# Extra products on TensorE in the first block of a pooled-attention and two-MLP kernel

## The chip, the cores and the metric

The kernel runs on one core of one Trainium2 chip, as one program with one launch. The metric is the device time of that program in microseconds (us): the median of several runs.

## The reference, cut to what matters

```python
# attention: q, k, v are (8, 8, 576, 64); keys and values are means over groups of 8 rows
k_p = k.reshape(B, H, Sp, pool, D).mean(axis=3)          # Sp = 72
v_p = v.reshape(B, H, Sp, pool, D).mean(axis=3)
scores = scale * np.matmul(q, k_p.transpose(0, 1, 3, 2))
attn = softmax(scores)                                    # over the 72 pooled keys
x = np.matmul(attn, v_p)  ->  (4608 tokens, 512)
# first MLP, three parallel inputs, d_ff = 768
h = np.maximum(np.maximum(x @ w1, x @ w2), x @ w3)
x = h @ w_out
# second MLP, d_ff = 2048
h = np.maximum(x @ w_in, 0.0)
return h * h @ w_out2
```

Here `softmax` and the last two names stand for a few lines of the reference. Inputs are float32; the weights of both MLPs come as 64-bit numbers.

## The kernel before, in words

**Tiling.** The 4608 tokens are cut into 12 blocks j of T1 = 384 tokens. For each block the kernel computes the attention of its tokens, which gives four tiles x[0] to x[3] (one for each pair of heads p), and then the first MLP in 22 steps: 18 steps (f, e), one for each of six column chunks f and three input weights e, and four output steps d. Nearly all products are made of split float32: a number is a high and a low part, and a product is three matmuls (high by high, high by low, low by high; PARTS in the code). So a step (f, e) is 4 x 3 = 12 matmuls of 384 columns (L465), and an output step is 18 (L484). The results wait in HBM for the second MLP, which runs after all blocks (L600 and L645).

**Attention of a block.** For each pair p: `prepare` makes the split queries and pooled keys, `softmax` multiplies queries by keys into a PSUM tile `sc` (L344), takes the maximum (VectorE, L346), exponentials (ScalarE, L349) and the division (GpSimd, L355). `transpose` then turns each tile of 128 queries round on TensorE (L370) into the PSUM tile `tr`, from which ScalarE (L372) and VectorE (L373) take the two parts `pt`. `values` multiplies by the pooled values (L385 for the first batch), and ScalarE (L121) and VectorE (L122) write the high and the low part of x[p]. In block 0 the query tiles of a pair start at c = 0, 128 and 256, so there are 12 transposed tiles. Pool `tr_ps` has one place for `tr`; the tile with c = 128 uses the place `av1` instead.

**Weights.** Each of the 18 input weights and six output weights of the first MLP is loaded by SyncE from HBM and turned from 64 bits into float32 with two ScalarE (L148, L149) and two VectorE (L150, L153) instructions, and then split (L121 on ScalarE, L122 on GpSimd). All of this happens while blocks 0 and 1 of the attention are made.

**Order.** Work goes into a list `todo` with a due time and is issued in that order; the attention of block j + 1 is spread over the steps of block j. The framework then places each engine's instructions by a timeline of its own (`schedule_with_timeline_sim=True`), with program order as priority, so an instruction that is ready can move ahead of one that isn't. On the chip every engine takes its instructions strictly in that placed order. `mm_ps` has three PSUM places, so three steps can be open at once.

Of the kernel before, what the change touches and what calls it, by code (L numbers as in the profile page):

```python
# [20 lines left out]
P = 128  # L21
B, H, S, D = 8, 8, 576, 64
POOL = 8
SP = S // POOL
# [8 lines left out]
NE = 3  # L33
# [32 lines left out]
NATURAL = 1  # L66

LIGHT = 2

# [8 lines left out]
def as_f32(ap):  # L80
    return ap.bitcast(F32)
# [3 lines left out]
def attention_moe_kernel(ctx: ExitStack, tc: tile.TileContext, q, k, v, vn, w1, w2, w3, wo1, wi2, wo2, out):  # L85
    nc = tc.nc
# [5 lines left out]
    ident = const.tile([P, P], F32, name="ident")  # L92
# [31 lines left out]
    def split(hl, src, engine=nc.vector):  # L124

        split_to(hl[:, 0], hl[:, 1], src, engine)
# [141 lines left out]
    def score_tiles(n):  # L268
        m = P if n % P == 0 else n // 2
        return [(c, m) for c in range(0, n, m)]  # L270

    def attention(j):
# [5 lines left out]
        for b, s0, n, t in pieces(j):  # L278
# [5 lines left out]
            for p in range(NPAIR):  # L284
# [3 lines left out]
                tiles = score_tiles(n)  # L288
                if j < LIGHT:
                    todo.append((at, functools.partial(softmax, tiles)))  # L290
                for c, m in tiles:
                    if j >= LIGHT:
                        todo.append((at, functools.partial(softmax, [(c, m)])))
# [13 lines left out]
    def attend(j, b, s0, n, p, t):  # L307

        kr, vr, qr, qs, pt, sms = [], [], [], [], [], {}
        first, light = s0 == 0, j < LIGHT  # L310

# [50 lines left out]
        def transpose(c, m):  # L362
            if c == 0:
                pt.append(pt_p.tile([SP, 2, 2, T1], F32R, tag="pt", name="pt"))
            if light and c == m:
                tr = av_ps.tile([P, T1], F32, tag="av1", name="tr")[:SP, : 2 * P].rearrange("s (h q) -> s h q", h=2)
            else:
                tr = tr_ps.tile([SP, 2, P], F32, tag="tr", name="tr")
            for h in range(2):
                nc.tensor.transpose(tr[:, h, :m], sms[c][:, h], ident[:m, :m])  # L370
            hi, lo = pt[0][:, 0, :, c : c + m], pt[0][:, 1, :, c : c + m]
            nc.scalar.activation(hi, tr[:, :, :m], AF.Copy)  # L372
            nc.vector.tensor_tensor(out=lo, in0=tr[:, :, :m], in1=as_f32(hi), op=ALU.subtract)  # L373

        def values():
# [24 lines left out]
            split(x, xf)  # L400

        return load, prepare, softmax, transpose, values

    w1_t, wo1_t = {}, {}
# [48 lines left out]
    def moe1(j):  # L453

        x = x_t.pop(j)
        hs = []
        for f in range(KF1):
            hm = t_p.tile([P, T1], F32, tag="hm", name="hm")
            h = h_p.tile([P, 2, T1], F32R, tag="h", name="h")
            for e in range(NE):  # L460
                ps = mm_ps.tile([P, T1], F32, tag="ps", name="ps")
                n = 0
                for kk in range(KD):
                    for a, c in PARTS:
                        nc.tensor.matmul(  # L465
                            ps, lhsT=w1_t[f, e][:, a, kk * P : (kk + 1) * P], rhs=x[kk][:, c],
                            start=(n == 0), stop=(n == 3 * KD - 1),
                        )
                        n += 1
                if e == 0:  # L470
                    nc.scalar.activation(hm, ps, AF.Copy)
                else:
                    nc.vector.tensor_tensor(out=hm, in0=ps, in1=hm, op=ALU.max)  # L473
                if e == NE - 1:
                    split(h, hm)
                yield
            hs.append(h)
            now[0] = hm
        for d in range(KD):
            ps = mm_ps.tile([P, T1], F32, tag="ps", name="ps")  # L480
            n = 0
            for kk in range(KF1):
                for a, c in PARTS:
                    nc.tensor.matmul(  # L484
                        ps, lhsT=wo1_t[kk][:, a, d * P : (d + 1) * P], rhs=hs[kk][:, c],
                        start=(n == 0), stop=(n == 3 * KF1 - 1),
                    )
                    n += 1
            ys = t_p.tile([P, T1], F32, tag="ys", name="ys")
            nc.scalar.activation(ys, ps, AF.Copy)  # L490
            nc.scalar.dma_start(out=y_dram[j][d], in_=ys)
            yield
# [6 lines left out]
    def add_moe1(j):  # L499
        steps = moe1(j)  # L500
        todo.extend((j * STEPS + i, functools.partial(next, steps, None)) for i in range(STEPS))
# [227 lines left out]
```

## Time and profile before

| | us |
|---|---|
| median of 3 runs | 1546.03 (1545.82 to 1547.47) |
| the profiled execution, its own time | 1546.39 |
| its span, first to last instruction | 1544.7 |
| TensorE busy in the span | 1509.4 (98%) |
| VectorE busy in the span | 948.2 (61%) |
| mean granted TensorE clock | 0.987 of full speed |

The profile is one execution. PE is TensorE, DVE is VectorE, ACT is ScalarE, POOL is GpSimd, SP is SyncE. L465 is line 465 of the kernel. A name such as `ps<-x,w` is the tile written and the tiles read. Times are counted from the span's start. The end of a matmul is modelled and overlaps the next one; the distance between two starts is what one costs in a row of them. A granted clock of 1.00 is 2.4 GHz and 0.50 is 1.2 GHz; those are the only two levels that this trace has. The first clock record is at 11.66 us; a stretch before it is printed as 1.00 whatever the clock was.

### The profile page before, as it was taken

How to read it: one execution, taken by the hardware profiler on the slowest of the kernel's cores; microseconds unless marked ns; L12 is line 12 of the kernel's file. 1: busy time of each engine (PE TensorE's matmuls, PEld its weight loads, DVE VectorE, ACT ScalarE, POOL GpSimd, SP SyncE). 2: the span in 40 equal slices, each digit the busy share in tenths (PEclk: the TensorE clock that was granted, in tenths of full speed). 3: DMA queues.
4: the chain of work that ended last, by engine and by line, in shares of the span. 5: the costliest groups of instructions: out<-in, count | busy, mean ns of one | idle time of the engine just before them, and what ended most of it. 6: DMA issues, size and time to landing. Idle time of an engine off the chain costs nothing.

```text
span 1544.7 us, 25098 instructions
## 1 busy us (share of the span) xinstructions
PE 1509.4 (98%) x9290; PEld 1413.8 (92%) x9290; DVE 948.2 (61%) x1991; ACT 623.5 (40%) x1772; POOL 199.4 (13%) x303
## 2 busy tenths in 40 slices
PE   6899999999999999999999999999999999999998
PEld 4789999999999999999999898988989888999987
DVE  6895678776776767755427555455655546464544
ACT  7875566656666556654212212121212112121211
POOL 5541122222222121322000000000000000000000
PEclk7799999999999999999999999999999999999999
DMA  7552234434334332323475424333333433343331
GB/s 226 159 172 68 76 105 149 145 95 143 122 119 143 97 132 99 102 77 123 135 289 208 150 109 164 110 121 123 112 137 124 150 123 108 111 150 109 137 109 69
DMA packets 80858, 200.87 MB, mean 130 GB/s; under 512 B 9024, under 2 KB 32576, under 8 KB 80736
## 3 DMA queue, kind: packets, MB, share of 16 engines
q1 hardware_dynamic: 73824, 189.83, 36.1%
q10 hardware_dynamic: 6912, 9.44, 1.7%
q8 instruction: 74, 1.21, 0.3%
q14 instruction: 48, 0.39, 0.1%
HBM read 157.29 MB, written 41.94 MB: 129 GB/s over the span
## 4 chain that ended last, share of the span: by engine, by line
PE 85%; DVE 5%; DMA 5%; ACT 2%; issue 2%; SPq 0%; POOL 0%; DVEq 0%; ACTq 0%; POOLq 0%
PE ps L465 25%; PE acc L645 25%; PE ps L600 21%; PE ps L484 9%; PE sc L344 2%; DMA out_dram<-o 2%; PE tr L370 2%; DMA wraw<-in_w_dram 1%; PE av L396 1%; PE av L395 1%; DVE wbits L153 1%; DMA vr<-in_v_dram 1%; DMA wraw<-in_wo_dram 1%; DMA kq<-in_k_dram 1%; DVE wbits L150 0%
## 5 line engine op out<-in xcount | busy, mean ns | idle before, releaser
L465 PE MATMUL ps<-x,w 128*128 128x384 f32 x2592 | 507.6, 343 | 1.8 <-DVE x L122 1.0
L465 PEld LDWEIGHTS ps<-x,w 128*128 128x128 f32 x2592 | 451.1, 191 | 3.9 <-DVE x L122 2.0
L645 PE MATMUL acc<-wo2s,g 128*128 128x512 f32 x1728 | 412.5, 391 | 0.0
L600 PEld LDWEIGHTS ps<-y,wi2s 128*128 128x128 f32 x3024 | 370.4, 188 | 12.5 <-PE ps L600 3.4
L600 PE MATMUL ps<-y,wi2s 128*128 128x256 f32 x3024 | 376.8, 280 | 2.8 <-DVE s L629 2.2
L645 PEld LDWEIGHTS acc<-wo2s,g 128*128 128x128 f32 x1728 | 316.2, 188 | 62.6
L121 ACT ACTIVATE g<-c 128x512 fp32r<-128x512 f32 x144 | 90.8, 630 | 410.4 <-DVE c L611 403.6
L617 DVE TENSOR_TENSOR s<-ps,s 128x512 f32<-128x512 f32 x72 | 49.8, 692 | 262.2 <-PE ps L600 261.6
L484 PE MATMUL ps<-h,wo 128*128 128x384 f32 x864 | 165.2, 339 | 0.5 <-DVE hm L473 0.4
L484 PEld LDWEIGHTS ps<-h,wo 128*128 128x128 f32 x864 | 148.9, 188 | 1.3 <-DVE hm L473 0.7
L617 DVE TENSOR_TENSOR c<-ps,s 128x512 f32<-128x512 f32 x144 | 99.0, 688 | 24.9 <-PE ps L600 21.7
L355 POOL TENSOR_TENSOR ss<-ss,st 128x144 f32<-128x144 f32 (+3 forms) x144 | 74.2, 517 | 308.7 <-DVE st L354 238.6
L473 DVE TENSOR_TENSOR hm<-ps,hm 128x384 f32<-128x384 f32 x144 | 79.5, 552 | 54.2 <-PE ps L465 50.3
L349 ACT ACTIVATE ss<-sc,st 128x72 f32<-128x72 f32 (+1 forms) x320 | 98.3, 314 | 33.3 <-DVE st L346 30.8
L122 DVE TENSOR_TENSOR g<-c,g 128x512 fp32r<-128x512 f32 x144 | 98.8, 686 | 17.3 <-ACT g L121 16.4
L611 DVE SCALAR_TENSOR_TENSOR c<-c 128x512 f32<-128x512 f32 x144 | 99.0, 688 | 2.2
L373 DVE TENSOR_TENSOR pt<-tr,pt 72x256 fp32r<-72x256 f32 (+1 forms) x160 | 61.5, 387 | 52.6 <-ACT pt L372 51.2
L344 PEld LDWEIGHTS sc<-kbd,qs 128*128 128x128 f32 (+1 forms) x480 | 73.3, 191 | 12.3 <-issue 5.3
L344 PE MATMUL sc<-kbd,qs 128*128 128x144 f32 (+1 forms) x480 | 73.9, 269 | 9.2 <-ACT kbd L195 5.3
L372 ACT ACTIVATE pt<-tr 72x256 fp32r<-72x256 f32 (+1 forms) x160 | 56.4, 355 | 58.9 <-PE tr L370 57.4
L370 PE MATMUL tr<-ident,ss 128*72 128x128 f32 (+1 forms) x320 | 59.2, 271 | 13.9 <-DVE pt L373 8.8
L349 ACT ACTIVATION_READ_ACCUMULATOR ss<-sc,st 128x1 f32 (+1 forms) x320 | 63.4, 198 | 0.0
(78 smaller groups left out, 1247.0 us busy)
## 6 DMA issues: line engine op xcount, KB each, us to landing
wo2s<-wo_dram SPq DMA_DIRECT2D x144, 512.0 KB
wi2s<-wi_dram SPq DMA_DIRECT2D x24, 512.0 KB
wraw<-in_wo_dram SPq DMA_DIRECT2D x22, 512.0 KB
wraw<-in_w_dram SPq DMA_DIRECT2D x18, 512.0 KB
y_dram<-ys ACTq DMA_DIRECT2D x48, 192.0 KB
out_dram<-o SPq DMA_DIRECT2D x36, 256.0 KB
wraw<-in_wi_dram SPq DMA_DIRECT2D x16, 512.0 KB
wi_dram<-wraw SPq DMA_DIRECT2D x16, 512.0 KB
```

What stands on the lines that cost most here:

```text
L121: nc.scalar.activation(hi, src, AF.Copy)
L122: engine.tensor_tensor(out=lo, in0=src, in1=as_f32(hi), op=ALU.subtract)
L344: nc.tensor.matmul(src[:, i], lhsT=lhsT, rhs=kbd[:, p, l], start=(n == 0), stop=(n == 2))
L349: nc.scalar.activation(ss[:, i, h], src[:, i, h], AF.Exp, bias=st[:, 0, i, h : h + 1], accum_out=st[:, 1, i, h : h + 1],)
L370: nc.tensor.transpose(tr[:, h, :m], sms[c][:, h], ident[:m, :m])
L465: nc.tensor.matmul(ps, lhsT=w1_t[f, e][:, a, kk * P : (kk + 1) * P], rhs=x[kk][:, c], start=(n == 0), stop=(n == 3 * KD - 1),)
L473: nc.vector.tensor_tensor(out=hm, in0=ps, in1=hm, op=ALU.max)
L484: nc.tensor.matmul(ps, lhsT=wo1_t[kk][:, a, d * P : (d + 1) * P], rhs=hs[kk][:, c], start=(n == 0), stop=(n == 3 * KF1 - 1),)
L600: nc.tensor.matmul(bank[:, u * HT : (u + 1) * HT], lhsT=wi2_t[2 * gr + u][i][:, a, o + kk * P : o + (kk + 1) * P], rhs=y_t[j][m][:, c, kk] ...
L611: nc.vector.scalar_tensor_tensor(out=c, in0=c, scalar=0.0, in1=c, op0=ALU.max, op1=ALU.mult)
L617: nc.vector.tensor_tensor(out=c, in0=bank, in1=other, op=ALU.add)
L645: nc.tensor.matmul(acc_t[j][2 * half + i], lhsT=g[:, a, u * HT + i * P : u * HT + (i + 1) * P], rhs=wo2_t[j, 4 * gr + 2 * u + h][:, c], st ...
```

## The change

In block 0 only, matmuls are added whose results are overwritten. `transpose` writes `ident` by `ident` into the place of the transposed tile ahead of the transposes: 14 times for the first tile, four times for each of the other 11. `moe1` writes, ahead of each step but the first, four products of the weight of the step before and x[0], both high parts, into the PSUM tile of the step. The real work that follows starts its sums anew.

```diff
+KEEP_T, KEEP_FIRST, KEEP_MAX = 4, 14, 4
...
                 tr = tr_ps.tile([SP, 2, P], F32, tag="tr", name="tr")
+            if j == 0:
+                for _ in range(KEEP_T if p or c else KEEP_FIRST):
+                    nc.tensor.matmul(tr[:, 0], lhsT=ident[:, :SP], rhs=ident, start=True, stop=True)
             for h in range(2):
                 nc.tensor.transpose(tr[:, h, :m], sms[c][:, h], ident[:m, :m])
...
                 ps = mm_ps.tile([P, T1], F32, tag="ps", name="ps")
+                if j == 0 and f + e:
+                    w = w1_t[divmod(NE * f + e - 1, NE)]
+                    for _ in range(KEEP_MAX):
+                        nc.tensor.matmul(ps, lhsT=w[:, 0, :P], rhs=x[0][:, 0], start=True, stop=True)
                 n = 0
                 for kk in range(KD):
```

## Rows read from the trace of the kernel before

**Rows 1.** The page: busy time of the engines, and the clock in 40 slices.

```profile
PE 1509.4 (98%) x9290; PEld 1413.8 (92%) x9290; DVE 948.2 (61%) x1991; ACT 623.5 (40%) x1772; POOL 199.4 (13%) x303
...
PEclk7799999999999999999999999999999999999999
```

**Rows 2.** Windows: length, busy us (instructions) by engine, clock, DMA share, GB/s.

```profile
21.90:49.20 27.30, 19.35 (x74) 16.28 (x74) 21.43 (x44) 21.95 (x79) 17.90 (x16) 0.50 0.60 181
49.20:59.45 10.25, 7.08 (x43) 5.11 (x41) 8.30 (x17) 9.52 (x34) 5.85 (x6) 1.00 0.63 216
59.45:66.28 6.83, 6.77 (x29) 6.14 (x30) 6.72 (x12) 6.83 (x25) 4.77 (x7) 0.50 0.32 98
103.82:107.23 3.41, 3.41 (x13) 3.12 (x14) 3.41 (x7) 3.27 (x14) 1.29 (x1) 0.50 0.55 143
```

```profile
66.50:115.10 48.60, 45.01 (x265) 42.16 (x263) 47.20 (x94) 36.61 (x106) 23.04 (x18) 0.96 0.53 172
126.70:1540.00 1413.30, 1406.75 (x8767) 1325.59 (x8767) 844.47 (x1776) 527.63 (x1455) 135.64 (x239) 1.00 0.37 126
```

**Rows 3.** The chain that ended last, at 115 us: start, length, what.

```profile
114.59 0.47 DVE hm L473
...
115.11 4.11 PE ps L484 x22
...
119.61 2.98 PE ps L484 x17
```

**Rows 4.** Timeline of TensorE: start, us, instruction, count, idle before it.

```profile
61.78 1.59 PE L385 MATMUL av<-pt,vst 72*128 72x192 f32 x6
63.17 2.18 PE L465 MATMUL ps<-x,w 128*128 128x384 f32 x6
65.14 0.84 PE L370 MATMUL tr<-ident,ss 96*72 96x96 f32 x4
65.69 0.98 PE L344 MATMUL sc<-kbd,qs 128*96 128x144 f32 x6
66.51 2.32 PE L465 MATMUL ps<-x,w 128*128 128x384 f32 x12
```

**Rows 5.** Timeline of VectorE: the low part of x[3].

```profile
61.20 0.52 DVE L122 TENSOR_TENSOR x<-av,x 128x384 fp32r<-128x384 f32 x1
```

**Rows 6.** Groups by line and shape on TensorE, 66.5 to 115.1 us.

```profile
L465 PE MATMUL ps<-x,w 128*128 128x384 f32 x180 | 35.5, 349 | 0.2
...
L484 PE MATMUL ps<-h,wo 128*128 128x384 f32 x15 | 3.0, 336 | 0.0
```

**Rows 7.** Waits of TensorE, 66.5 to 115.2 us: total, times, longest.

```profile
PE av L395 <- DVE xf L399: 2.1, 1, 2.1
PE tr L370 <- DVE pt L373: 0.5, 1, 0.5
PE ps L484 <- DVE hm L473: 0.4, 1, 0.4
```

**Rows 8.** Waits of VectorE and ScalarE for TensorE, 14 to 60 us.

```profile
DVE st L346 <- PE sc L344: 1.2, 1, 1.2
```

```profile
ACT x L121 <- PE av L385: 0.9, 1, 0.9
ACT pt L372 <- PE tr L370: 0.5, 1, 0.5
```

**Rows 9.** Waits of TensorE, 14 to 60 us.

```profile
PE tr L370 <- DVE pt L373: 6.8, 4, 3.6
```

**Rows 10.** Timelines of GpSimd and TensorE at the start.

```profile
3.52 0.29 POOL masks.py:199 TENSOR_SCALAR_AFFINE_SELECT ident<-ident 128x128 f32<-128x128 f32 x1
```

```profile
5.35 0.46 PE L344 MATMUL sc<-kbd,qs 128*128 128x144 f32 x1 [5.35 <-ACT kbd L195]
...
8.36 6.27 PE L250 MATMUL vp<-natural,sums 128*72 128x512 f32 x10
14.56 1.71 PE L344 MATMUL sc<-kbd,qs 128*128 128x144 f32 x11
16.10 0.60 PE L370 MATMUL tr<-ident,ss 128*72 128x128 f32 x4
```

## The prediction

> **What bounds the kernel now.** I read the page first. TensorE is busy for 98% of the span, and its clock is below full only in the first two of the 40 slices [rows 1]. So the body of the kernel is limited by TensorE, and the change can only act at the start. The windows say where the start ends: from 126.7 us to 1540 us TensorE is busy for 1406.75 of 1413.30 us [rows 2]. Any microsecond by which TensorE comes later to the end of block 0 is therefore added to the whole, and any that it gains there is saved whole.
>
> Next I cut the first 115 us at the clock's changes. There are three stretches at half clock: 21.90 to 49.20 us, 59.45 to 66.28 us and 103.82 to 107.23 us [rows 2]. In the first, TensorE is busy for only 19.35 of 27.30 us, while VectorE, ScalarE and GpSimd have 21.43, 21.95 and 17.90 us of work: the attention of block 0 and the conversion of the weights share these engines. There TensorE waits for the others, and a slow clock costs little. From 66.5 to 115.1 us it is different: TensorE is busy for 45.01 and VectorE for 47.20 of 48.60 us [rows 2]. Both are nearly full. The chain that ended last runs through VectorE up to its maximum at 114.59 us and through TensorE from 115.11 us on [rows 3].
>
> The point between these two regimes is the low part of x[3], the last that the first steps need: VectorE writes it from 61.20 to 61.72 us [rows 5]. Up to there the three open steps can only go as far as x goes. From 66.51 us on whole steps of 12 matmuls run [rows 4].
>
> **The change, part by part. The products ahead of the steps.** There are 17 x 4 = 68 matmuls of 384 columns. One costs what its neighbours cost: 17 in 2.98 us at full clock, 0.175 us each [rows 3]; at half clock six took 63.17 to 65.14 us, 0.33 us each [rows 4]. The products of steps 1 and 2 can run while TensorE waits for x, because three PSUM places are open from the start: nothing (1.4 us if that cover were gone). The 15 other steps run in 66.5 to 115.1 us, which is 180 matmuls of L465 [rows 6]. Their 60 products stand in TensorE's queue ahead of real work: 60 x 0.175 = 10.5 us.
>
> What can pay for them there? The real work needs 195 x 0.175 us for L465 and L484, and the other 70 instructions some 0.09 us each (16 of them took 2.76 us at half clock, 61.78 to 63.17 and 65.14 to 66.51 us [rows 4]): 34.1 + 6.3 = 40.4 of 48.6 us. So 8.2 us are not used. Of these, three waits for VectorE make 3.0 us [rows 7]; a TensorE that arrives later no longer meets them. The half clock of 103.82 to 107.23 us costs half of 3.41 us, 1.7 us; it follows the longest of these waits (2.1 us), and goes with it. The remaining 3.5 us are changes of shape and small gaps, which I leave as they are.
>
> **The products ahead of the transposes.** A product of `ident` is plain float32 like those of L250, which are five in the code and ten in the trace, so each becomes two instructions. These ten took 6.20 us (8.36 to 14.56 us), of which 3.30 us before the clock rose at 11.66 us: with c for one at half clock, 3.30/c + 2.90/(c/2) = 10, so c = 0.91 us for 512 columns [rows 10]. A product of 128 columns is then 2 x 0.23 = 0.46 us at half clock and 0.23 us at full; the trace has none, so this is an estimate. Four cost 0.9 us at full clock and 1.8 at half; the 44 after the first tile 10 to 20 us, all before 60 us.
>
> Bounds of what they do: above, they stand between the release of the `tr` place and the transposes. Four transposes waited for that release [rows 9], and if all 11 tiles were delayed by 0.9 us with the chain behind them, x[3] would come 10 us later. Below, they keep the clock up, and the waits that VectorE and ScalarE spend on TensorE before 60 us go: 1.2 + 0.9 + 0.5 = 2.6 us [rows 8]. I take zero, nearer the lower end: a tile that left TensorE mostly waits for ScalarE and VectorE, which have other work queued, and gain and delay are of one size there. The first 14 can start when `ident` is ready at 3.81 us; at half clock they take 6.4 us, and the first scores, at 5.35 us, may come up to 4 us later [rows 10]. The first transpose ran only at 16.10 us [rows 10], so I cost this at nothing too.
>
> **What the clock gives back.** After x[3] is complete at 61.72 us, TensorE needs from 61.78 to 66.51 us at half clock for what then stands before step 3 [rows 4]. At full clock that is half: 2.4 us gained.
>
> The Trainium skill (TensorE: Matmul & The Clock Gate, Why this matters for your kernels) advises against pauses between bursts of matmuls, since the clock falls back after them; the same page (Part 1) puts the loss by warming up at under 1% of a typical span, which would be some 15 us here. The rows allow 9.7 + 3.4 + 1.7 = 14.8 us, half of the busy time in the three slow stretches [rows 2], but only if TensorE were the limit in all of them.
>
> **Sum.** + 10.5 - 2.4 - 3.0 - 1.7 + 0 = + 3.4 us. The profiled execution took 1546.39 us, 1.7 us beside its span, and the median is 1546.03 us; the difference doesn't matter. I predict 1549 us. If none of the waits goes, it is 10.5 - 2.4 = + 8.1 us; if all of the 8.2 us go, it is - 0.1 us. So the case's own range is 1546 to 1554 us.
>
> **Rivals.** First, faster: the clock is worth more than I allow. If the products hold the clock up through 21.90 to 49.20 us and TensorE does stand in the chain to x[3], up to half of its 19.35 busy us, 9.7 us, comes off: 3.4 - 9.7 = - 6.3 us, 1540 us. It decides from the point at which x[3] is complete 6.5 us sooner, before 55 us. For it: TensorE works at half clock there for 27.30 us [rows 2], and a softmax passes it three times. Against: only 2.6 us of waits on it are to be seen on VectorE and ScalarE [rows 8], and VectorE, which is full from 59.45 us on, would have to be early as well. 24%.
>
> Second, slower than I say: the products hold up the transposes. With half of the bound, 5 us, on x[3], the sum is + 8.4 us, 1554 to 1555 us, and with the whole 1559 us. For it: the one place for `tr` and the four waits for it [rows 9], in an order that is fixed before the run. Against: the clock should be full then, and ScalarE and VectorE are often late anyway. 20%.
>
> Third, no difference: VectorE is the limit up to 115.11 us, and the products fill only time in which TensorE would have waited for it, so that all 8.2 us are used: 1546 us. For it: VectorE's 47.20 of 48.60 us. Against: TensorE waits for it by name only 3.0 us [rows 7]. 12%.
>
> **How the numbers follow.** My case has 44%. About 0.2%, 3.1 us, is what a measurement of this kernel tells from no change. Of my case's range a little less than half lies within that: 20% same, 24% slower. The first rival is faster (24%, and 1% for an order of instructions that happens to be better), the second slower (20%), the third the same (12%, small change). Together 25% faster, 32% same, 43% slower. The range for 8 in 10 goes from the first rival's 1540 us to 1557 us, inside the second's end.
>
> **What the profile after would show.** If I am right: no half clock between 59 and 110 us; step 3 starting 2 to 3 us sooner; the wait of 2.1 us before L395 gone; TensorE at 100% from there; and the first L484 of block 0 some 3 us later than now. If the first rival holds, x[3] is complete before 55 us. If the second holds, it is complete after 64 us, with transposes that follow their products without a gap. I would also be wrong if the framework placed the instructions of the other engines in another order, since its timeline sees the new products, and the start has many queues that wait for each other.

## The result, and the profile after

The changed kernel is slower: 1555.91 us median (1554.61 to 1560.07) against 1545.92 us, a ratio of 1.0072 with a 95% interval of 1.0057 to 1.0088. The direction and the range for 8 in 10 held, the size did not: 10 us (11 us by the ratio) instead of 3.4, and the time lies above the 1546 to 1554 us of my own case.

The profiled execution took 1558.67 us, 2.8 us over the median, with a span of 1557.0 us. The page after, busy time and clock in 40 slices, answers to [rows 1]:

```profile
PE 1524.3 (98%) x9474; PEld 1434.7 (92%) x9474; DVE 948.1 (61%) x1991; ACT 624.6 (40%) x1772; POOL 191.5 (12%) x303
...
PEclk8899999999999999999999999999999999999999
```

184 matmuls more: 68 ahead of the steps and 58 pairs ahead of the transposes. The windows after (length, busy us and count of TensorE, its weight loads, VectorE, ScalarE and GpSimd, then clock, DMA share and GB/s) answer to [rows 2]:

```profile
17.89:28.13 10.24, 7.22 (x34) 6.91 (x35) 8.85 (x18) 10.15 (x40) 7.21 (x7) 0.50 0.51 156
45.20:48.61 3.41, 3.09 (x13) 2.52 (x12) 2.76 (x3) 3.38 (x14) 3.03 (x3) 0.50 0.71 203
62.27:69.09 6.82, 6.10 (x24) 5.46 (x25) 6.74 (x15) 5.73 (x23) 4.19 (x5) 0.50 0.49 150
99.81:106.64 6.83, 6.01 (x19) 6.01 (x20) 6.31 (x11) 5.79 (x18) 2.69 (x2) 0.50 0.52 140
71.40:128.20 56.80, 52.55 (x308) 50.59 (x307) 45.98 (x97) 38.26 (x113) 20.74 (x17) 0.94 0.43 129
142.50:1553.00 1410.50, 1403.74 (x8764) 1323.30 (x8763) 845.80 (x1779) 527.86 (x1462) 129.47 (x239) 1.00 0.37 126
```

Half clock before 110 us fell from 37.5 to 27.3 us, and the kernel is slower all the same. The stretch of the steps is not fuller: TensorE is idle for 4.25 us of 56.80 (3.59 of 48.60 us before). From 142.5 us on the body is as full as before. Waits of TensorE, 60 to 130 us, answer to [rows 7]:

```profile
PE tr L378 <- DVE pt L381: 3.4, 3, 1.3
PE av L403 <- DVE pt L381: 1.2, 1, 1.2
PE ps L473 <- ACT hm L483: 0.8, 1, 0.8
PE av L393 <- DVE x L127: 0.7, 1, 0.7
PE sc L349 <- ACT ss L354: 0.7, 1, 0.7
PE av L403 <- DVE x L127: 0.2, 1, 0.2
```

That is 7.0 us of waits where I expected none of these to be left. The timelines of VectorE (the low part of x[3]) and TensorE, which answer to [rows 5] and [rows 4]; L473 is an added product, L477 the real work of a step and L496 the output step:

```profile
64.68 0.54 DVE L127 TENSOR_TENSOR x<-av,x 128x384 fp32r<-128x384 f32 x1
```

```profile
70.62 0.97 PE L473 MATMUL ps<-x,w 128*128 128x384 f32 x4 [0.77 <-ACT hm L483]
71.43 2.07 PE L477 MATMUL ps<-x,w 128*128 128x384 f32 x11
...
128.17 1.20 PE L496 MATMUL ps<-h,wo 128*128 128x384 f32 x6
...
142.52 2.32 PE L477 MATMUL ps<-x,w 128*128 128x384 f32 x12
```

x[3] is complete 3.5 us later (65.22 against 61.72 us), the real work of step 3 starts 4.9 us later, the first output matmul of block 0 comes at 128.17 us, where it stood at 111.53 us before, and block 1 starts at 142.52 instead of 126.69 us: 15.8 us late. The end is only some 10 us late, so part of this is given back later.

### The profile page after: what moved, and what is told of

Read it like the earlier page. It is cut to its first block, busy times and chain, and to the rows that moved or that the text cites. A ratio compares the mean times of both kernels' runs of the same rounds, so it can differ in the third digit from the quotient of the medians.

```text
span 1557.0 us, 25422 instructions
## 1 busy us (share of the span) xinstructions
PE 1524.3 (98%) x9474; PEld 1434.7 (92%) x9474; DVE 948.1 (61%) x1991; ACT 624.6 (40%) x1772; POOL 191.5 (12%) x303
## 4 chain that ended last, share of the span: by engine, by line
PE 53%; DMA 3%; DVE 1%; issue 0%; ACT 0%; SPq 0%; DVEq 0%; ACTq 0%
PE acc L657 24%; PE ps L612 20%; PE ps L477 5%; PE ps L496 2%; DMA out_dram<-o 2%; DVE c L629 0%; DMA wo2s<-wo_dram 0%; DVE s L641 0%; PE tr L378 0%; ACT o L669 0%; PE sc L349 0%; PE av L403 0%; PE av L404 0%; SPq L670 0%; DVE s L629 0%
## 5 line engine op out<-in xcount | busy, mean ns | idle before, releaser
L477 PE MATMUL ps<-x,w 128*128 128x384 f32 x2592 | 504.7, 342 | 0.6 <-ACT x L126 0.6
L477 PEld LDWEIGHTS ps<-x,w 128*128 128x128 f32 x2592 | 449.3, 190 | 1.4 <-ACT x L126 0.9
L496 PE MATMUL ps<-h,wo 128*128 128x384 f32 x864 | 164.3, 339 | 0.0
L496 PEld LDWEIGHTS ps<-h,wo 128*128 128x128 f32 x864 | 148.8, 188 | 0.0
L360 POOL TENSOR_TENSOR ss<-ss,st 128x144 f32<-128x144 f32 (+3 forms) x144 | 70.0, 487 | 381.2 <-DVE st L359 285.7
L127 DVE TENSOR_TENSOR g<-c,g 128x512 fp32r<-128x512 f32 x144 | 98.7, 686 | 17.6 <-ACT g L126 16.7
L380 ACT ACTIVATE pt<-tr 72x256 fp32r<-72x256 f32 (+1 forms) x160 | 56.4, 353 | 53.7 <-PE tr L378 51.7
L349 PEld LDWEIGHTS sc<-kbd,qs 128*128 128x128 f32 (+1 forms) x480 | 69.9, 184 | 1.6 <-ACT ss L354 0.9
L351 DVE TENSOR_REDUCE st<-sc 128x2 f32<-128x144 f32 (+3 forms) x144 | 45.4, 316 | 38.0 <-PE sc L349 35.5
L126 ACT ACTIVATE h<-hm 128x384 fp32r<-128x384 f32 x72 | 37.7, 523 | 68.3 <-DVE hm L485 67.8
```

Source lines behind the costliest of these rows:

```text
L126: nc.scalar.activation(hi, src, AF.Copy)
L127: engine.tensor_tensor(out=lo, in0=src, in1=as_f32(hi), op=ALU.subtract)
L349: nc.tensor.matmul(src[:, i], lhsT=lhsT, rhs=kbd[:, p, l], start=(n == 0), stop=(n == 2))
L360: nc.gpsimd.tensor_tensor(out=ss, in0=ss, in1=st[:, 2].rearrange("p g (h o) -> p g h o", o=1).to_broadcast([m, g, 2, SP]), op=ALU.mult,)
L477: nc.tensor.matmul(ps, lhsT=w1_t[f, e][:, a, kk * P : (kk + 1) * P], rhs=x[kk][:, c], start=(n == 0), stop=(n == 3 * KD - 1),)
L496: nc.tensor.matmul(ps, lhsT=wo1_t[kk][:, a, d * P : (d + 1) * P], rhs=hs[kk][:, c], start=(n == 0), stop=(n == 3 * KF1 - 1),)
```

## The experiments

Times are medians in us; each ratio is to runs of the kernel before on the same chip, with its 95% interval. "Block 1" is the start of its first step's matmul in the profile, which is one execution; in the kernel before it is 126.7 us.

**The parts of the change, each alone.** The three constants select them:

```diff
-KEEP_T, KEEP_FIRST, KEEP_MAX = 4, 14, 4
+KEEP_T, KEEP_FIRST, KEEP_MAX = 0, 0, 4     # e1, and e4 with the condition below
+KEEP_T, KEEP_FIRST, KEEP_MAX = 4, 14, 0    # e2
+KEEP_T, KEEP_FIRST, KEEP_MAX = 0, 14, 0    # e3
...
-                if j == 0 and f + e:
+                if j == 0 and 0 < NE * f + e < 3:   # e4
```

e1, the steps alone:

> Only the four products ahead of each step of block 0, none ahead of the transposes. Theory A (the 60 products of steps 3 to 17 stand in TensorE's queue in front of real work and are paid in full, 60 x 0.175 = 10.5 us): the first L484 of block 0 comes 10 to 13 us later than before and the whole is 8 to 12 us slower than before. Theory B (the products ahead of the transposes are what costs, by a later x[3]): 0 to 4 us slower. Theory C (the other order in which the framework places all engines' instructions moves the time, whatever the products last): any value, also outside these two.

e2, the transposes alone:

> Only the products ahead of the transposes (14 and 11 x 4), none ahead of the steps. Theory A: within 2 us of before, x[3] complete at 62 to 65 us and step 3 soon after. Theory B: 5 to 10 us slower than before, with x[3] 4 us or more late and that delay kept to the end. Theory C: any value, and a sum with the run of the steps alone that is not the whole change's 10 us.

e3, the first tile's 14 alone:

> Only the 14 products ahead of the very first transposed tile, 28 instructions before 10 us. Theory A and B: no effect beyond 2 us, as TensorE waits for other engines until 60 us. Theory C: the order of all engines differs from before here too, so some us either way are possible; more than 3 us could only be order.

e4, steps 1 and 2 alone:

> Only the products ahead of steps 1 and 2, eight matmuls of 384 columns, 1.4 us at full clock, which run while TensorE waits for x[1]. Theory A and B: the same time as before within 1 us. Theory C: some us either way although the added work is all hidden.

| | median | ratio (95% interval) | block 1 at |
|---|---|---|---|
| e1 steps only | 1553.44 | 1.0033 (1.0021 to 1.0046) | 137.6 |
| e2 transposes only | 1546.68 | 0.9996 (0.9987 to 1.0006) | 132.0 |
| e3 first tile only | 1548.59 | 1.0008 (0.9998 to 1.0018) | 132.9 |
| e4 two steps only | 1548.98 | 1.0010 (1.0000 to 1.0019) | 128.6 |

The parts don't add to the whole: 0.33% and -0.04% against 0.72%. At the start of block 1 they do: 10.9 and 5.3 us late, 16.2 together, against 15.8, but each of these builds has an order of its own, so this can be chance. e1's first output step is 11.2 us late, as theory A said, and its time (5.1 us) lies in neither theory's range; e2's time is theory A's, its late block 1 is not. And e3 is the odd one: 28 instructions, the last of which ends at 15.5 us, make block 1 6.2 us late, and then nearly all of it comes back (5.3 us in one block, around 500 us; more on that below). Neither theory A nor B has a place for that. Between these builds not only the products differ: the framework placed the instructions of the engines anew (place by place in the traces, VectorE's order in e3 differs from that of the kernel before at 1144 of 1991 instructions). So theory C had to be tested by itself.

**The order held.** The kernel is built twice in one run of its host code. The first build gives the order in which the framework placed everything; the second adds the products, and each engine's other instructions are tied to that order by edges that fix the issue order and make nothing wait. In the traces of e5, e6, e7 and e9 the instructions of TensorE, VectorE, ScalarE and GpSimd, products left out, then follow one another as in the kernel before, without one difference in operation, tile or shape; those of e8 as in the changed kernel.

```diff
+            traced = [i for i in traced if i.name not in extra]      # without the added products
+            for k in order:
+                i = traced[k]
+                before = at.get(i.engine)
+                if before is not None:
+                    tc.add_manual_dep(i, before.name, DependencyInfo(NoSync, DATA), reason="order")
+                at[i.engine] = i
...
+    nc, maps, names = build((0, 0, 0))
+    place = {n: k for k, n in enumerate(names)}
+    order = [place[i.name] for i in nc.all_instructions() if i.name in place]
+    nc, maps, _ = build((0, 0, 4), order)     # e5; e6 (4, 14, 0), e7 (4, 14, 4), e9 (0, 0, 8)
```

For e8 the first build has (4, 14, 4) and the second (0, 0, 0): the changed kernel's order without a product.

> Only the products ahead of the steps, with every other instruction of every engine held in the order of the kernel before. Theory A (paid in full on TensorE, and the run of the steps alone gave back 5 to 6 us in block 3 only because its other order has no stall there): the first L484 of block 0 is 9 to 12 us late, the stall near 500 us is there again, and the whole is 9 to 12 us slower than before. Theory D (the give-back belongs to the delay itself: a TensorE that is late meets no stall in block 3): 4 to 6 us slower, as with the order left free.

> Only the products ahead of the transposes, every other instruction held in the order of the kernel before. If these products cost nothing themselves and the 5 us that TensorE lost by 130 us in the run of the transposes alone came from the order: within 2 us of before. If they hold up the transposes (theory B): x[3] complete 3 us or more later and 4 to 6 us slower.

> All added products, every other instruction held in the order of the kernel before. Theory A: 10 to 12 us slower, the steps' products alone. Theory B: 14 to 17 us slower, both kinds. If the order of the changed kernel is what hurts most: under 8 us.

> No added product; every instruction held in the order of the changed kernel. Theory A with the order as a second cause: TensorE loses some 5 us more by 130 us than before, has no stall in block 3, and the whole is within 2 us of before. Theory C (the order is what costs): 5 us or more slower. If the new order is only the windfall of block 3: 4 to 6 us faster.

> Eight products ahead of each step instead of four, none ahead of the transposes, every other instruction in the order of the kernel before. Theory E (in the old order TensorE's unused time takes up most of the first 10.5 us, 7.8 us by the run with four, and then there is none left): the next 10.5 us are paid nearly in full, 9 to 11 us slower than with four, 1559 to 1562 us. If VectorE were the limit all along, the next four would again cost 3 to 4 us: 1553 to 1555 us.

| | median | ratio (95% interval) | block 1 at |
|---|---|---|---|
| e5 steps, old order | 1550.51 | 1.0028 (1.0019 to 1.0037) | 129.1 |
| e6 transposes, old order | 1548.66 | 1.0012 (1.0002 to 1.0021) | 128.6 |
| e7 all, old order | 1552.47 | 1.0030 (1.0018 to 1.0042) | 132.0 |
| e8 no product, new order | 1555.29 | 1.0056 (1.0044 to 1.0068) | 138.5 |
| e9 eight a step, old order | 1560.57 | 1.0085 (1.0071 to 1.0098) | 140.2 |

This tells the two apart. The order of the changed kernel costs 0.56% (8.7 us) without one added product; all the products in the old order cost 0.30% (4.6 us). No run holds the old order without a product, which would show whether holding costs anything by itself; the nearest is e12 below, whose first 300 us are just that, and its block 1 starts at 125.6 us, 1.1 us sooner than before.

Theory A fails for e5: its 60 products were not paid in full. (Its 4.3 us are in theory D's range, but theory D's reason is not there: the wait near 500 us came back, as shown further down.) The windows of e5 show why, from 49.3 us to the end of the steps:

```profile
49.30:56.10 6.80, 4.65 (x26) 3.30 (x26) 6.30 (x14) 6.59 (x21) 2.96 (x4) 1.00 0.56 192
56.10:66.30 10.20, 10.20 (x47) 9.59 (x48) 8.96 (x19) 9.88 (x38) 7.75 (x9) 0.50 0.46 153
66.50:115.10 48.60, 48.60 (x306) 48.45 (x306) 46.93 (x90) 36.13 (x104) 21.22 (x18) 1.00 0.53 173
```

In 66.5 to 115.1 us TensorE is busy for all of 48.60 us with 306 instructions, at full clock; it was 45.01 us with 265 at 0.96 [rows 2]. Its first output matmul starts at 114.60 us, 3.1 us later than before, so 7.4 of the 10.5 us of products don't show there: 0.35 us because step 3 starts sooner, the other 7.1 went into time that was not used. At the end e5 is 4.3 us late. The second MLP, which has no product, takes 762.9 us in its profile and 760.1 in that of the kernel before (760 to 764 us over all profiles); what moves it is not shown, so differences of 2 to 3 us at the end are not shown to come from block 0. In e9, TensorE's timeline has that point at 125.71 us:

```profile
125.71 1.55 PE L498 MATMUL ps<-h,wo 128*128 128x384 f32 x8
```

So the second four a step cost 11.1 us there (0.8 of it before step 3) and 0.57% (8.8 us) in the end, near the 9 to 11 us of theory E: here, when the cover was used up, a product cost its duration.

The waits of TensorE in e8, 60 to 130 us, have no product in them (in these builds L380 is the transpose, L383 VectorE taking its part, L479 a step, L498 the output step and L129 the low part of x):

```profile
PE tr L380 <- DVE pt L383: 4.9, 5, 1.9
PE av L395 <- DVE x L129: 2.2, 2, 1.6
PE av L405 <- DVE pt L383: 1.9, 1, 1.9
PE tr L380 <- POOL ss L362: 0.7, 1, 0.7
PE ps L479 <- ACT hm L485: 0.6, 1, 0.6
PE tr L380 <- DVE st L360: 0.5, 1, 0.5
PE av L405 <- DVE x L129: 0.2, 1, 0.2
```

11.0 us of waits, against 3.3 us before (3.0 of it in [rows 7]; the fourth wait is 0.3 us). Five transposes wait 4.9 us in total for VectorE to read the one `tr` place, one did for 0.5 us before. The timelines of e8, VectorE's first, show x[3], the start of step 3, the worst place and the first output matmul:

```profile
66.23 0.54 DVE L129 TENSOR_TENSOR x<-av,x 128x384 fp32r<-128x384 f32 x1
```

```profile
72.29 2.20 PE L479 MATMUL ps<-x,w 128*128 128x384 f32 x11 [0.60 <-ACT hm L485]
...
98.65 0.33 PE L380 MATMUL tr<-ident,ss 96*72 96x96 f32 x2 [1.91 <-DVE pt L383]
98.77 0.42 PE L479 MATMUL ps<-x,w 128*128 128x384 f32 x1
101.13 0.36 PE L405 MATMUL av<-pt,vst 72*128 72x192 f32 x1 [1.94 <-DVE pt L383]
...
124.17 1.20 PE L498 MATMUL ps<-h,wo 128*128 128x384 f32 x6
```

Before, two tiles were transposed together, as at 65.14 us [rows 4]; here one tile stands alone, and TensorE waits for VectorE ahead of it, to free the place, and again behind it, for VectorE's part of the turned tile. These waits are only a part of the loss. Step 3 starts 5.8 us later than before, with x[3] 5.1 us late, and from there to the first output matmul it is 51.9 us against 45.0. Half clock before 110 us is 51.2 us in e8, against 37.5; how much of the late x[3] is due to that, these runs don't separate.

**One side held.** In e10 only TensorE's order is held, in e11 only that of the four others; all products are in.

```diff
                 i = traced[k]
+                if i.engine != EngineType.PE:     # e10; == in e11
+                    continue
```

> All added products; TensorE's other instructions are held in the order of the kernel before, and the other engines' are left to the framework. If TensorE's own order (where the transposes stand) is what the new order costs: 3 to 6 us slower than before, as with all engines held. If the order of VectorE, ScalarE and the loads is what costs: 8 us or more.

> All added products; VectorE, ScalarE, GpSimd and SyncE are held in the order of the kernel before, and TensorE's order is left to the framework. If TensorE's own order costs: 8 us or more slower than before. If the others' order costs: 3 to 6 us.

e10: 1562.11, 1.0095 (1.0081 to 1.0108), 14.7 us, in the range for the other engines' order. e11: 1555.57, 1.0049 (1.0035 to 1.0063), 7.6 us, in neither range. Both mixtures are slower than the old order throughout (e7, 1.0030; e11 by little over the intervals), and e10 is slower than the new order throughout (e8). But the side left free didn't get the changed kernel's order: VectorE's in e10 differs from that at 1143 of 1991 instructions and from the old one at 181, and TensorE's in e11 from the old one at 204 of 9290. So these are two further orders. They show that holding one side alone is not enough; which engine's order makes the changed kernel slow, and whether it is how the orders fit each other, they don't show.

**Where in the order.** Two orders are joined at a cut: the first n instructions as placed from one, the rest as in the other.

```diff
+    head = old[:3000]                        # e12, e16; e13 new[:3000], e14 new[:450], e15 old[:450]
+    kept = set(head)
+    nc, maps, _ = build((0, 0, 0), head + [k for k in new if k not in kept])   # e16: (4, 14, 4)
```

> No added product; the first 3000 placed instructions (to some 300 us) in the order of the kernel before, the rest in the order of the changed kernel, which has no stall in block 3. If that stall belongs to the order alone: TensorE loses under 1 us between 480 and 520 us instead of 4.9 us, and the kernel is 3 to 5 us faster than before, a version that beats both. If the stall follows from how early block 0 ends: the same time as before.

> No added product; the first 3000 placed instructions in the order of the changed kernel, the rest in that of the kernel before. If the new order's loss (11 us by 130 us) and its gain in block 3 (5 to 6 us) are separate and add: 11 to 14 us slower than before, with the stall near 500 us. If the stall vanishes because block 0 ends late: 7 to 9 us slower, as with the new order throughout.

> No added product; the first 450 placed instructions (to some 60 us in the kernel before) in the order of the changed kernel, the rest in that before. If the loss is made after 60 us, where TensorE has no cover: 1 to 4 us slower than before. If the front's order costs (a later x[3] that VectorE never makes good): 8 us or more.

> No added product; the first 450 placed instructions in the order of the kernel before, the rest in that of the changed kernel. If the loss is made between 60 and 130 us: 9 us lost there less 5 us of block 3, 3 to 6 us slower than before. If it is made in the front: 3 to 6 us faster than before.

> All added products; the first 3000 placed instructions in the order of the kernel before, the rest in that of the changed kernel. If products and order add: 4 to 5 us for the products less 5 to 6 us of block 3, within 2 us of before, and some 10 us faster than the changed kernel with the same products.

| | median | ratio (95% interval) | block 1 at |
|---|---|---|---|
| e12 old to 300 us, then new | 1541.58 | 0.9962 (0.9949 to 0.9976) | 125.6 |
| e13 new to 300 us, then old | 1559.90 | 1.0082 (1.0069 to 1.0095) | 138.0 |
| e14 new to 60 us, then old | 1550.71 | 1.0023 (1.0014 to 1.0031) | 131.0 |
| e15 old to 60 us, then new | 1555.05 | 1.0047 (1.0035 to 1.0059) | 138.0 |
| e16 as e12, all products | 1547.34 | 1.0002 (0.9993 to 1.0010) | 130.4 |

The new order has a loss and a gain, and they are separate. Its first 300 us cost 0.82% (12.7 us, e13); the rest gains 0.38% (5.9 us, e12). Their sum, 6.8 us, agrees with e8's 8.7 us within the intervals. The gain lies around 500 us, in block 7 by the starts of the steps (the expectations call it block 3). From its start to that of block 8 it is 59.6 to 59.7 us in the profiles of the changed kernel, e1, e2, e3, e8, e12, e15 and e16, and 63.8 to 66.2 us in the ten others, among them every one with the old order after 300 us. TensorE's timeline of the kernel before has a wait there, with half clock behind it (3.41 us from 499.8 us); the second fence is that of e5:

```profile
498.29 1.16 PE L344 MATMUL sc<-kbd,qs 128*128 128x144 f32 x6 [1.89 <-ACT ss L349]
```

```profile
500.90 1.16 PE L351 MATMUL sc<-kbd,qs 128*128 128x144 f32 x6 [1.89 <-ACT ss L356]
```

In e5 the clock stays at 1.00 behind the same wait, and block 7 is 1.2 us shorter than before. The windows around it, first of the kernel before and then of e12:

```profile
480.00:530.00 50.00, 47.83 (x286) 46.39 (x285) 36.00 (x98) 32.00 (x107) 11.91 (x21) 0.97 0.39 129
```

```profile
480.00:530.00 50.00, 48.96 (x301) 48.24 (x301) 35.55 (x96) 31.24 (x100) 12.12 (x21) 1.00 0.38 128
```

Fifteen matmuls more in the same 50 us. e13, whose block 1 is as late as e8's but whose later order is the old one, has the wait of 1.9 us again, so it belongs to the order and not to when block 0 ends. e12 is faster than both kernels.

The early loss is not in one place. The new front alone costs 0.23% (3.6 us, e14). The new order from 60 us on, taken without the gain that e12 shows, costs 0.47% + 0.38% = 0.85% (13 us, e15). These make 1.08% (16.7 us), more than the 0.82% of e13 by little over the intervals; at block 1 it is 4.3 + 11.3 = 15.6 us against 11.3. So the joint at 60 us seems to have a price of its own, and how the loss divides stays open. The expectation for e15 (3 to 6 us) was too low, its time is 7.3 us: VectorE completes x[3] at 61.1 us there, but TensorE then waits 2.8 us for VectorE and 3.1 us for ScalarE, and step 3 starts at 71.5 us.

e16 closes the account: all products, in the old order to 300 us and the new one after it, come out even with the kernel before, 0.70% (11 us) better than the changed kernel with the same products. e7's 0.30% and e12's -0.38% would give -0.08%, as measured within the intervals.

## Why the prediction was wrong

**What bounds the kernel: right.** TensorE fills the body as before, and a delay of block 0 goes to the end where the later order is the same (e7: 5.3 us at block 1, 4.6 us in the time). In the changed kernel 15.8 us at block 1 became 10, and 5.4 us of it came back in block 7 by the other order.

**The products ahead of the steps: right in size, and mostly covered.** 0.175 us each held: in e9 60 more of them took 10.3 us from step 3 on, once nothing covered them. I took 4.7 us of the 8.2 us of unused time as cover (3.0 of waits, 1.7 of clock). In e5 these waits and that half clock are gone, as I had said, but the cover is 7.1 us.

**The clock gives back 2.4 us: failed.** In e5 the clock was at half from 56.10 to 66.30 us; what stands between the end of x[3] and step 3 took 4.9 us (61.23 to 66.16 us), against 4.7 before. Step 3's first product starts 0.35 us sooner than step 3 did before, and x[3] is complete 0.55 us sooner there. The two errors, 2.4 us too little cover and 2.0 us too much clock, nearly cancel, which is luck.

**The products ahead of the transposes, costed at nothing: too low by some 2 us.** Their price was right: eight instructions from 24.23 to 25.98 us at half clock are 0.44 us a product, from 35.47 to 36.34 us at full clock 0.22 us; I had 0.46 and 0.23:

```profile
24.23 1.95 PE L376 MATMUL tr<-ident 128*72 128x128 f32 x8 [2.74 <-DVE pt L381]
25.98 0.63 PE L378 MATMUL tr<-ident,ss 128*72 128x128 f32 x2
...
35.47 1.04 PE L376 MATMUL tr<-ident 128*72 128x128 f32 x8
36.34 0.38 PE L378 MATMUL tr<-ident,ss 128*72 128x128 f32 x2
```

In the old order they delay x[3] by 2.4 us (VectorE's L129 from 63.56 to 64.08 us in e6) and the end by 0.12% (1.9 us, with an interval of 0.3 to 3.2).

**The sum, for the order that I had read: near.** 3.4 us predicted, 4.6 us (2.8 to 6.5) measured in e7, with the two errors above inside it.

**The step that failed: the sum had no term for the order.** It was made on the queues of the kernel before, with the products put in between. The prediction names another order as something that could happen, but gave it 1% and only as a gain. The new order alone costs 8.7 us (e8), most of the change's 11 us; by the ratios of e8 and of the change the products add 0.16% (2.5 us), which the intervals don't tell from nothing. Even 14 products that end by 15.5 us changed the order of all four engines compared (e3). Four draws of an order (e1 to e4) and the change's own make block 1 late by 1.9 to 15.8 us; all the products in the old order make it 5.3 us late (e7). Why the framework's timeline placed them so is open.

**The rivals.** The first, that the clock is worth more, fell: there are 10 us less of half clock, and the kernel is slower; e7, in the order of the kernel before, has only 13.7 us of it before 130 us, x[3] later and a longer time. The second seemed confirmed by its sign, x[3] complete after 64 us, and by the time; but in e8, with no product at all, x[3] is complete at 66.77 us. So the new order gives that sign by itself. In the old order e6 shows this rival's delay at 2.4 us, half of the 5 us that it asked for. The third fell, as e7 is slower clear of the interval; its cover, all 8.2 us, was nearer to the 7.1 us of e5 than mine.

Of the rule in the Trainium skill (TensorE: Matmul & The Clock Gate, Why this matters for your kernels), that pauses between bursts cost the clock, the rows agree as far as the products held the clock: in e7 it is at full from 39.7 us to 130 us.

```profile
39.70:130.00 90.30, 84.05 (x543) 80.52 (x542) 77.60 (x161) 66.95 (x215) 43.33 (x37) 1.00 0.49 152
```

But it didn't pay here: between 60 and 130 us TensorE waited for 2.9 us, little less than the 3.3 us before, and the kernel was slower.

## What to carry to other kernels

Where a scheduler places the instructions by a timeline of its own, an edit can redraw the order of all engines, as the change and e1 to e4 did here. The new order cost 8.7 us, and its later part alone gained 5.9 us, against 4.6 us for the edit itself, so give the order a term in the sum, with both signs, and measure it by holding the order. Read a change's cost at the point where its cover ends, too: at the first output step 7.4 of 10.5 us of products were free, and of the next 10.5 us none. And a stall that vanishes after an edit somewhere else (here at 500 us) is a finding by itself: keep it and drop the edit.

## What the runs showed of the hardware that I had not expected

The granted clock can be at half while TensorE is full: in e5 it is 0.50 from 56.10 to 66.30 us, with TensorE busy for 10.20 of 10.20 us. It had been at full in the 6.80 us ahead of that, with TensorE busy for 4.65 us. In the kernel before it is 0.50 from 59.45 to 66.28 us, with TensorE busy for 6.77 of 6.83 us [rows 2]. In both cases the stretch ahead of the fall was the less busy one (7.08 of 10.25 us before [rows 2]), so in these rows the fall goes with what came before it and not with the work under it. A pause doesn't always bring it: behind the wait of 1.89 us near 500 us it fell in the kernel before and not in e5. What brings it back after 10.20 us of full work, and after 6.83 us in the kernel before [rows 2], these runs don't show.
